# Batch 0's key-value products by head pairs, idle products in float32, and a second pair normalised on GpSimd

## The chip, the cores and the metric

The kernel runs on one core of one Trainium2 chip. The metric is the device time of one execution in microseconds (us); a lower one is better. A core has five engines that run their own instruction streams and wait for each other through semaphores: TensorE (PE in the profile, with its weight loads as PEld), VectorE (DVE), ScalarE (ACT), GpSimd (POOL) and SyncE (SP). Sixteen transfer engines (DMA) move data between memory and the core; transfers issued by SyncE are the queue "q1 hardware_dynamic" in the profile, those issued by GpSimd "q0 software_dynamic".

## The reference

Linear attention over 8 batches of 8 heads, 576 positions and 64 channels, followed by a two-layer network with a leaky ReLU, all in float32 at the interface:

```python
q_s = softmax of q over the channels
k_s = softmax of k over the positions
kv = np.einsum('bhsd,bhse->bhde', k_s, v)
x = np.einsum('bhsd,bhde->bhse', q_s, kv)        # (8, 8, 576, 64) -> tokens (4608, 512)
h = x @ w_in                                     # (512, 2048)
g = np.maximum(0.01 * h, h)
out = g @ w_out                                  # (2048, 512)
```

## The kernel before, in words

The 4608 tokens are worked off in nine tiles of 512. For each tile, 16 blocks of layer 1 (`layer1`, L521: four products over the channel blocks cb 0 to 3 of `w_in_sb`) are evicted through the leaky ReLU on ScalarE (L530), and then layer 2 (L542) multiplies them with `w_out_sb`. The attention of batch b+1 is prepared under the products of tile b, at places written out by hand with `at(tile, unit, ...)`. The order of instructions on every engine is the order of the program; nothing is rescheduled.

The change lies in the part before the first tile, L576 to L632, where batch 0's attention has nothing to hide under, and in `x1` at L771. A batch's eight heads lie in four pairs of partition halves: `hl` counts four heads per half, and a "pair" gg takes heads 2gg and 2gg+1 (called hp 0 and 1) in each of the two partition halves hh. One position row r of the nine holds 64 positions per half.

What is issued there, in order:

- SyncE loads q's first four rows (`RA`), k in two halves, v in two halves, and q's other rows (L93 to L96).
- `wake` and `wake_on` (L344, L350) run products on zeros or on a small tile, whose results nobody reads, into a PSUM tile of their own. `wake(14)` is first; others fill waits between the steps.
- GpSimd issues the first half of w_in (1024 of its 2048 columns, four pieces of 256 KB as stored, one for each cb) once k has landed: `load_w_in(0)`, L579. It casts v's first half (L593), normalises q's first rows of pair 0 (`q_first_norm`, L602), and then issues the second half of w_in, `load_w_in(1)`, L603.
- k's maximum over the positions goes through VectorE and TensorE (`k_tree`, `k_max_pe`, `k_all_dve`, `k_all_pe`), is subtracted (`k_sub_ps`, VectorE), and ScalarE takes the exponentials into `ke`.
- `kv_pair` (L389) multiplies `ke` with v, which carries a column of ones, for both heads and both halves: `kv_quads` issues, for each of nine rows, four products of 64 positions x 64 channels with 65 columns. The two results `pkv[hh]` lie in two PSUM banks, the two heads in the two halves of the partitions. The column of ones gives k's sum; `kd_rec` takes its reciprocal and `kd_one` writes the normalised result to `kd2` (VectorE).
- `q_turn_first` transposes q's first rows of a pair on TensorE, `q_keep_first` copies them to `qT`, `attend` (L444) multiplies with `kd2` and `x_keep` copies the result to `xT`, layer 1's input. Channel blocks 0 and 1 come from pair 0, blocks 2 and 3 from pair 1.
- For pair 0 VectorE keeps the transposes, for pair 1 ScalarE. Pair 1 is normalised on VectorE (L618).
- `q_max` and `q_sub` begin the softmax of rows 4 and 5 (`R1`) and 6 and 7 (`R2`), VectorE and GpSimd.

Then the first half (256 tokens) of tile 0 begins (L778 on): for the first eight blocks of layer 1 all products with cb 0, then `x1` (the attend of pair 1, its `x_keep`, and the exponentials of R1), then cb 1, 2 and 3. The other eight blocks need the second half of w_in; between their cb 0, 1 and 2 stand the transposes of R2's rows (`t2`), an attend of rows 4 to 7 (`x2`) and the first block of the second half of the tokens.

SyncE's next loads, batch 1's k and q, wait for the first piece of w_in's second half: `hold_sync(0, ...)` at L635 reads it first. GpSimd's later issues of w_out (`late_loads`, L640) wait for its third piece.

PSUM has eight banks: six rotate under one tag (`psB_pool`), two under another (`psO_pool`).

Of the kernel before, what the change touches and what calls it, by code (L numbers as in the profile page):

```python
# [8 lines left out]
FP32 = mybir.dt.float32  # L9
# [11 lines left out]
R = 9  # L21
# [4 lines left out]
def kernel(  # L26
# [68 lines left out]
    st[0]["v"] = load(v, 0, "v_raw", [(slice(0, 2), ALLR), (slice(2, 4), ALLR)])  # L95
    load(q, 0, "q_raw", [(ALLH, RB)], st[0]["q"])  # L96

    zero = const_pool.tile([P, TT], BF16)
    nc.gpsimd.memset(zero, 0.0)  # L99
    ident = const_pool.tile([P, P], BF16)  # L100
    make_identity(nc, ident)
# [9 lines left out]


    vb2 = [const_pool.tile([P, R, 2, 2, D + 2], BF16, name=f"vb{i}") for i in range(2)]
    kd2 = [const_pool.tile([P, 2, 2, D], BF16, name=f"kd{i}") for i in range(2)]
    for i in range(2):
        nc.gpsimd.memset(vb2[i][:, :, :, :, D : D + 1], 1.0)
# [1 line left out]

    w_in_r = moe_w_in.rearrange("(cb p) f -> p cb f", p=P)

    def load_w_in(fh):
        fs = slice(fh * (F // 2), (fh + 1) * (F // 2))
        for cb in range(NB):
            nc.gpsimd.dma_start(out=w_in_sb[:, cb, fs], in_=w_in_r[:, cb, fs])  # L124

    w_out_r = moe_w_out.rearrange("(fb f) o -> f fb o", f=P)
# [182 lines left out]
    def kv_quads(b, gg, outs, rs=ALLR):  # L309
        for r in range(R)[rs]:  # L310
            for hp in range(2):
                for hh in range(2):
                    rows = slice(hh * L, (hh + 1) * L)
                    nc.tensor.matmul(  # L314
                        outs[hh][hp * D : (hp + 1) * D, 0 : D + 1],
                        lhsT=st[b]["ke"][rows, r, 2 * gg + hp],
                        rhs=vb2[b % 2][rows, r, gg, hp, 0 : D + 1],
                        start=(r == 0),
                        stop=(r == R - 1),
                    )  # L320
# [20 lines left out]

    wake_ps = psO_pool.tile([P, TT], FP32, name="pout", tag="pout")

    def wake(n):  # L344
        for i in range(n):
            nc.tensor.matmul(  # L346
                wake_ps, lhsT=zero[:, 0:P], rhs=zero, start=(i == 0), stop=(i == n - 1)
            )

    def wake_on(a, n):  # L350
        for i in range(n):
            nc.tensor.matmul(
                wake_ps[0:RA.stop, 0:P], lhsT=a[:, HL - 1], rhs=identf, start=True, stop=True
            )

    def k_max_pe(b, i):
        ps = psB_pool.tile([P, 2, L], FP32, name="kT", tag=BANK_TAG)
# [28 lines left out]
        )  # L386

    def kv_pair(b, gg):
        pkv = [psB_pool.tile([P, D + 2], FP32, name="pkv1", tag=BANK_TAG) for _ in range(2)]  # L389
        kv_quads(b, gg, pkv)  # L390
        st[b]["pkv", gg] = pkv

    def kd_rec(b, gg, hh):
        st[b]["krec", gg, hh] = krec = small_pool.tile([P, 1], FP32, name="krec1")
        nc.vector.reciprocal(out=krec, in_=st[b]["pkv", gg][hh][:, D : D + 1])

    def kd_one(eng, b, gg, hh):
        pkv, krec = st[b]["pkv", gg][hh], st[b]["krec", gg, hh]
        eng.tensor_tensor(
            out=kd2[b % 2][:, gg, hh], in0=pkv[:, 0:D], in1=krec.to_broadcast([P, D]), op=ALU.mult  # L400
        )

    def q_transpose(b, r0, n, pool=psB_pool, tag=BANK_TAG):
# [22 lines left out]
    def cross(b, gg, outs, rows):  # L426
        for hp in range(2):
            for hh in range(2):
                half = slice(hp * D, (hp + 1) * D)
                if b == 1 and rows.start == RE.start:  # L430
                    rhs = st[b]["qE"].rearrange("c (r g) (h l) -> c g h r l", g=2, h=2)[:, gg, hh]
                elif "qX" in st[b]:
                    rhs = st[b]["qX"].rearrange("c (r g) (h l) -> c g h r l", g=2, h=2)[:, gg, hh, rows]
                else:
                    rhs = st[b]["qT"][:, 2 * hh + gg, rows]
                nc.tensor.matmul(  # L436
                    outs[hp][hh * D : (hh + 1) * D].rearrange("p (r l) -> p r l", l=L),
                    lhsT=kd2[b % 2][half, gg, hh],
                    rhs=rhs[half],
                    start=True,  # L440
                    stop=True,
                )
# [131 lines left out]


    HA, HB = slice(0, 1), slice(1, 2)  # L576
    wake(14)
    nc.gpsimd.tensor_copy(out=gate[:, 0:1], in_=st[0]["k"][:, HL - 1, R - 1, D - 1 : D])
    load_w_in(0)  # L579
    k_begin(0)  # L580
    q_begin(0)
    q_first(0, RA)
    wake_on(st[0]["nmax"], 4)
    k_tree(0, H0)
    k_max_pe(0, 0)
    wake(1)
    k_tree(0, H1, slice(0, 1))
    k_all_dve(0, 0)
    k_all_pe(0, 0)
    wake(2)  # L590
    k_tree(0, H1, slice(1, 4))
    nc.gpsimd.tensor_copy(out=gate[:, 0:1], in_=st[0]["kmax"][:, HL - 1, D - 1 : D])
    v_cast(nc.gpsimd, 0, 0)  # L593
    k_max_pe(0, 1)
    wake(1)
    k_sub_ps(0, 0, HA)
    k_exp(0, slice(0, 1))
    k_all_dve(0, 1)
    k_all_pe(0, 1)
    wake(3)  # L600
    q_first_rec(0, 0)
    q_first_norm(nc.gpsimd, 0, 0)  # L602
    load_w_in(1)  # L603
    k_sub_ps(0, 0, HB)
    k_exp(0, slice(1, 2))
    v_cast(nc.scalar, 0, 1)
    q_first_rec(0, 1)
    k_sub_ps(0, 1)
    k_exp(0, H1)
    kv_pair(0, 0)  # L610
    q_turn_first(0, 0)
    wake(3)
    kd_rec(0, 0, 0)
    kd_one(nc.vector, 0, 0, 0)
    q_keep_first(nc.vector, 0, 0)
    kd_rec(0, 0, 1)
    kd_one(nc.vector, 0, 0, 1)
    q_first_norm(nc.vector, 0, 1)  # L618
    attend(0, (0,), RA)
    for hp in range(2):  # L620
        x_keep(nc.scalar, 0, (0,), RA, hp)
    kv_pair(0, 1)
    q_turn_first(0, 1)
    q_keep_first(nc.scalar, 0, 1)
    q_max(0, R1)
    q_sub(nc.gpsimd, 0, R1)
    for hh in range(2):
        kd_rec(0, 1, hh)
        kd_one(nc.vector, 0, 1, hh)
    q_max(0, R2)  # L630
    q_sub(nc.gpsimd, 0, R2)
    load_w_out(slice(0, 2))  # L632


# [124 lines left out]
    def end_act(j, ph, half):  # L759
# [10 lines left out]
    )  # L770
    x1 = (  # L771
        lambda: attend(0, (1,), RA),
        lambda: x_keep(nc.vector, 0, (1,), RA, 0),
        lambda: q_exp(0, R1),
        lambda: x_keep(nc.scalar, 0, (1,), RA, 1),
    )

# [93 lines left out]
```

## The time and the profile before

| | us |
|---|---|
| median of 3 runs | 282.64 (282.36 to 283.31) |
| the profiled execution | 282.63 |
| its span, first to last instruction | 280.8 |

| engine | busy us | share of the span | instructions |
|---|---|---|---|
| TensorE, products | 273.7 | 97% | 2018 |
| TensorE, weight loads | 133.0 | 47% | 2018 |
| VectorE | 159.9 | 57% | 227 |
| ScalarE | 160.3 | 57% | 284 |
| GpSimd | 51.6 | 18% | 52 |

The granted clock of TensorE is 1.00 in every slice of the span. The transfer engines are busy 90% or more from about 7 us on in the first sixth of the span. Rows of the profile name an instruction by its line, engine and operation, the tile written and the tiles read, the sizes, how often it ran, and its mean time; the chain that ended last is followed back from the last instruction, at each step to what released it.

### The profile page before, as it was taken

The numbers are of one execution on the slowest core, as the hardware profiler recorded it, in microseconds if no ns is written. First come the engines' busy times: TensorE is split into PE (matmuls) and PEld (weight loads), VectorE is DVE, ScalarE is ACT, GpSimd is POOL, SyncE is SP. The second block draws the span as 40 slices with busy tenths as digits, with TensorE's granted clock in tenths as the row PEclk, the third lists the DMA queues.
The fourth block names the chain that finished last, engine by engine and source line by source line (L and its number), as shares of the span: only waits on it lengthen the run. The fifth ranks groups of instructions, "written<-read, shape, count | busy, mean of one in ns | idle before, by whom it ended". The sixth has DMA issues, their size and how long they took to land.

```text
span 280.8 us, 5005 instructions
## 1 busy us (share of the span) xinstructions
PE 273.7 (97%) x2018; PEld 133.0 (47%) x2018; DVE 159.9 (57%) x227; ACT 160.3 (57%) x284; POOL 51.6 (18%) x52
## 2 busy tenths in 40 slices
PE   8889999999999999999999999999999999999994
PEld 3378645444444544444444444444444444444443
DVE  3985897999999959956895598644600000000021
ACT  4975565784489177755586448644844364146400
POOL 2947280159005003000400070000000000000000
PEclk9999999999999999999999999999999999999999
DMA  7999999896692498099309930332033300330033
GB/s 246 332 209 319 247 261 398 265 377 198 194 396 94 90 362 292 1 255 394 92 2 255 400 84 0 84 77 58 20 84 75 71 6 0 75 77 0 0 75 77
DMA packets 37751, 45.94 MB, mean 164 GB/s; under 512 B 16608, under 2 KB 20960, under 8 KB 37728
## 3 DMA queue, kind: packets, MB, share of 16 engines
q1 hardware_dynamic: 34240, 41.30, 46.5%
q0 software_dynamic: 3328, 4.20, 8.5%
q8 instruction: 16, 0.26, 0.4%
q10 hardware_dynamic: 160, 0.13, 0.2%
q14 instruction: 7, 0.06, 0.1%
HBM read 36.70 MB, written 9.44 MB: 164 GB/s over the span
## 4 chain that ended last, share of the span: by engine, by line
PE 92%; DMA 5%; POOL 2%; SPq 0%; issue 0%; DVE 0%
PE pout L542 45%; PE ph L521 43%; DMA w_in_sb<-in_moe_w_in_dram 3%; DMA k_raw<-in_k_dram 2%; PE po L436 1%; PE pokv L314 1%; PE pkv L314 1%; POOL w_in_sb L124 1%; POOL vb L204 0%; SPq L81 0%; POOL qe L243 0%; PE psum_q L254 0%; PE pokv L436 0%; PE psum_qt L407 0%; DVE out_sb L536 0%
## 5 line engine op out<-in xcount | busy, mean ns | idle before, releaser
L542 PE MATMUL pout<-w_out_sb,gj 128*128 128x512 bf16 (+2 forms) x592 | 127.9, 374 | 0.0
L521 PE MATMUL ph<-xT,w_in_sb 128*128 128x512 bf16 (+1 forms) x640 | 126.6, 358 | 0.7 <-DMA w_in_sb<-in_moe_w_in_dram 0.7
L530 ACT ACTIVATE gj<-ph 128x512 bf16<-128x512 f32 x144 | 82.0, 602 | 26.9 <-PE ph L521 26.5
L521 PEld LDWEIGHTS <-w_in_sb 128*128 128x128 bf16 x640 | 62.3, 98 | 63.0 <-DMA w_in_sb<-in_moe_w_in_dram 0.9
L542 PEld LDWEIGHTS <-gj 128*128 128x128 bf16 x592 | 56.4, 98 | 64.9 <-issue 0.2
L536 ACT COPY out_sb<-pout 128x512 f32<-128x512 f32 (+1 forms) x29 | 16.8, 580 | 67.0 <-PE pout L542 46.2
L536 DVE COPY out_sb<-pout 128x512 f32<-128x512 f32 (+1 forms) x8 | 4.8, 638 | 70.8 <-PE pout L542 70.8
L204 POOL CAST vb<-v_raw 128x1152 bf16<-128x1152 f32 x13 | 22.8, 1781 | 81.3 <-DMA v_raw<-in_v_dram 67.0
L294 DVE TENSOR_REDUCE qsum<-qe 128x36 f32<-128x2304 bf16 (+5 forms) x13 | 20.0, 1541 | 9.8 <-ACT qe L285 9.6
L192 ACT ACTIVATE ke<-k_raw 128x2304 bf16<-128x2304 f32 (+2 forms) x11 | 17.6, 1598 | 10.8 <-DVE k_raw L184 10.7
L301 DVE TENSOR_TENSOR qe<-qe,qrec 128x2304 bf16<-128x2304 bf16 (+5 forms) x13 | 22.4, 1724 | 0.4
L215 DVE TENSOR_REDUCE qmax<-q_raw 128x36 f32<-128x2304 f32 (+5 forms) x13 | 20.0, 1537 | 0.7 <-DMA q_raw<-in_q_dram 0.7
L285 ACT ACTIVATE qe<-q_raw 128x2304 bf16<-128x2304 f32 (+5 forms) x13 | 17.2, 1320 | 3.0 <-POOL q_raw L277 3.0
L184 DVE TENSOR_TENSOR k_raw<-k_raw,kall 128x2304 f32<-128x2304 f32 (+1 forms) x8 | 17.2, 2164 | 0.3
L277 POOL TENSOR_TENSOR q_raw<-q_raw,qmax 128x512 f32<-128x512 f32 (+3 forms) x7 | 11.9, 1697 | 23.9 <-DVE qmax L215 19.1
L459 ACT CAST xT<-po 128x512 bf16<-128x512 f32 (+3 forms) x34 | 15.3, 540 | 1.5 <-PE po L436 1.5
L151 DVE TENSOR_TENSOR t<-t 128x256 f32<-128x256 f32 (+2 forms) x22 | 15.5, 706 | 0.7
L151 DVE TENSOR_TENSOR t<-k_raw 128x512 f32<-128x512 f32 (+1 forms) x11 | 12.1, 1102 | 2.2 <-DMA k_raw<-in_k_dram 1.9
L277 DVE TENSOR_TENSOR q_raw<-q_raw,qmax 128x2304 f32<-128x2304 f32 (+1 forms) x6 | 13.2, 2203 | 0.3
L334 DVE RECIPROCAL krec<-pokv 128x2 f32<-128x2 f32 x8 | 1.3, 165 | 20.8 <-PE pokv L436 20.8
L346 PE MATMUL pout<-zero 128*128 128x512 bf16 x24 | 8.4, 492 | 1.3 <-POOL zero L99 1.3
L314 PEld LDWEIGHTS <-ke 64*64 64x64 bf16 x576 | 6.7, 107 | 4.6 <-issue 2.5
(68 smaller groups left out, 106.4 us busy)
## 6 DMA issues: line engine op xcount, KB each, us to landing
out_dram<-out_sb SPq DMA_DIRECT2D x70, 128.0 KB, 2.9
q_raw<-in_q_dram SPq DMA_DIRECT2D x6, 1152.0 KB, 8.5
v_raw<-in_v_dram SPq DMA_DIRECT2D x6, 1152.0 KB, 11.0
k_raw<-in_k_dram SPq DMA_DIRECT2D x5, 1152.0 KB, 6.1
k_raw<-in_k_dram SPq DMA_DIRECT2D x6, 576.0 KB, 5.5
v_raw<-in_v_dram SPq DMA_DIRECT2D x4, 576.0 KB, 7.6
w_in_sb<-in_moe_w_in_dram POOLq DMA_DIRECT2D x8, 256.0 KB, 7.7
w_out_sb<-in_moe_w_out_dram POOLq DMA_DIRECT2D x8, 256.0 KB, 10.6
```

The lines of the kernel that those rows point to most:

```text
L151: nc.vector.tensor_tensor(out=o, in0=i0, in1=i1, op=ALU.max)
L184: eng.tensor_tensor(out=ks, in0=ks, in1=st[b]["kall"][:, hs].unsqueeze(2).to_broadcast([P, n, R, D]), op=ALU.subtract,)
L192: nc.scalar.activation(out=st[b]["ke"][:, :, hs].rearrange("p r h d -> p h r d"), in_=st[b]["k"][:, hs], func=AF.Exp,)
L204: eng.tensor_copy(out=o, in_=i)
L215: nc.vector.tensor_reduce(out=o, in_=st[b]["q"][:, hs, rs], axis=AX.X, op=ALU.max)
L277: eng.tensor_tensor(out=qs, in0=qs, in1=st[b]["qmax", rs.start, hs.start].unsqueeze(3).to_broadcast([P, m, n, D]), op=ALU.subtract,)
L294: nc.vector.reduce_sum(out=qsum, in_=st[b]["qe"][:, rs, hs], axis=AX.X)
L301: nc.vector.tensor_tensor(out=qes, in0=qes, in1=st[b]["qrec", rs.start, hs.start].unsqueeze(3).to_broadcast([P, n, m, D]), op=ALU.mult,)
L521: nc.tensor.matmul(ph, lhsT=w_in_sb[:, cb, j * P : (j + 1) * P], rhs=xT[:, cb, c0 : c0 + n], start=(cb == 0 and first), stop=(cb == NB - 1 ...
L530: nc.scalar.activation(out=o, in_=ph, func=AF.Prelu, alpha=LEAKY_SLOPE)
L536: copy(out=out_sb, in_=pout)
L542: nc.tensor.matmul(pout, lhsT=g_sb[j // 2][:, j % 2, tsub * P : (tsub + 1) * P], rhs=w_out_sb[:, j, os], start=(j == 0), stop=(j == NF - 1),)
```

## The change

- `zero` becomes a float32 tile of 128 columns. `wake` takes the numbers of columns of the float32 products that it runs, each reading one zero column again and again: 512, 512, 512 and 256 in place of 14 bf16 products of 512; 128, 256 and 384 in place of one, two and three. `wake_on` runs one float32 product of 512 columns in place of four of 128.
- `kv_pair` multiplies both heads of a pair at once: 64 positions x 128 channels with 130 columns, 18 products in place of 36 for each pair. Half of the result (one head's k with the other's v) is not used. `kd_one` normalises all of it into a tile of its own, `kd0`, and batch 0's attend reads the fitting quarter. Later batches go on with `kd2`.
- Pair 1 of q's first rows is normalised on GpSimd directly after pair 0, ahead of the issues of w_in's second half. These are split: pieces 0 and 1 there, piece 2 after `q_sub` of R1, piece 3 after `q_sub` of R2.
- R1's `q_max` and `q_sub`, pair 1's transposes and their copy (now VectorE) stand ahead of pair 0's `x_keep` and of `kv_pair(0, 1)`.
- In `x1` both `x_keep` are ScalarE's, and the exponentials of R1 stand ahead of them.

```diff
-    zero = const_pool.tile([P, TT], BF16)
+    zero = const_pool.tile([P, P], FP32)
...
+    kd0 = const_pool.tile([P, 2, 2, 2, D], BF16)
...
-    def load_w_in(fh):
+    def load_w_in(fh, cbs=slice(0, NB)):
         fs = slice(fh * (F // 2), (fh + 1) * (F // 2))
-        for cb in range(NB):
+        for cb in range(NB)[cbs]:
             nc.gpsimd.dma_start(out=w_in_sb[:, cb, fs], in_=w_in_r[:, cb, fs])
...
-    def wake(n):
-        for i in range(n):
+    def wake(*cols):
+        for n in cols:
             nc.tensor.matmul(
-                wake_ps, lhsT=zero[:, 0:P], rhs=zero, start=(i == 0), stop=(i == n - 1)
+                wake_ps[:, 0:n], lhsT=zero, rhs=zero[:, 0:1].to_broadcast([P, n]), start=True, stop=True
             )
 
-    def wake_on(a, n):
-        for i in range(n):
-            nc.tensor.matmul(
-                wake_ps[0:RA.stop, 0:P], lhsT=a[:, HL - 1], rhs=identf, start=True, stop=True
-            )
+    def wake_on(a):
+        nc.tensor.matmul(
+            wake_ps[0 : RA.stop], lhsT=a[:, HL - 1], rhs=zero[:, 0:1].to_broadcast([P, TT]), start=True, stop=True
+        )
...
     def kv_pair(b, gg):
-        pkv = [psB_pool.tile([P, D + 2], FP32, name="pkv1", tag=BANK_TAG) for _ in range(2)]
-        kv_quads(b, gg, pkv)
+        pkv = [psB_pool.tile([P, 2, D + 2], FP32, name="pkv1", tag=BANK_TAG) for _ in range(2)]
+        for r in range(R):
+            for hh in range(2):
+                rows = slice(hh * L, (hh + 1) * L)
+                nc.tensor.matmul(
+                    pkv[hh][:, :, 0 : D + 1],
+                    lhsT=st[b]["ke"][rows, r, 2 * gg : 2 * gg + 2].rearrange("p h d -> p (h d)"),
+                    rhs=vb2[b % 2][rows, r, gg, :, 0 : D + 1],
+                    start=(r == 0),
+                    stop=(r == R - 1),
+                )
...
-        nc.vector.reciprocal(out=krec, in_=st[b]["pkv", gg][hh][:, D : D + 1])
+        nc.vector.reciprocal(out=krec, in_=st[b]["pkv", gg][hh][:, 0, D : D + 1])
...
         eng.tensor_tensor(
-            out=kd2[b % 2][:, gg, hh], in0=pkv[:, 0:D], in1=krec.to_broadcast([P, D]), op=ALU.mult
+            out=kd0[:, gg, hh],
+            in0=pkv[:, :, 0:D],
+            in1=krec.unsqueeze(2).to_broadcast([P, 2, D]),
+            op=ALU.mult,
         )
...
-                    lhsT=kd2[b % 2][half, gg, hh],
+                    lhsT=kd0[half, gg, hh, hp] if b == 0 else kd2[b % 2][half, gg, hh],
...
-    wake(14)
+    wake(TT, TT, TT, 256)
...
-    wake_on(st[0]["nmax"], 4)
+    wake_on(st[0]["nmax"])
...
     q_first_norm(nc.gpsimd, 0, 0)
-    load_w_in(1)
     k_sub_ps(0, 0, HB)
     k_exp(0, slice(1, 2))
     v_cast(nc.scalar, 0, 1)
     q_first_rec(0, 1)
+    q_first_norm(nc.gpsimd, 0, 1)
+    load_w_in(1, slice(0, 2))
     k_sub_ps(0, 1)
     k_exp(0, H1)
     kv_pair(0, 0)
     q_turn_first(0, 0)
-    wake(3)
+    wake(384)
     kd_rec(0, 0, 0)
     kd_one(nc.vector, 0, 0, 0)
     q_keep_first(nc.vector, 0, 0)
     kd_rec(0, 0, 1)
     kd_one(nc.vector, 0, 0, 1)
-    q_first_norm(nc.vector, 0, 1)
     attend(0, (0,), RA)
+    q_max(0, R1)
+    q_sub(nc.gpsimd, 0, R1)
+    load_w_in(1, slice(2, 3))
+    q_turn_first(0, 1)
+    q_keep_first(nc.vector, 0, 1)
     for hp in range(2):
         x_keep(nc.scalar, 0, (0,), RA, hp)
     kv_pair(0, 1)
-    q_turn_first(0, 1)
-    q_keep_first(nc.scalar, 0, 1)
-    q_max(0, R1)
-    q_sub(nc.gpsimd, 0, R1)
     for hh in range(2):
         kd_rec(0, 1, hh)
         kd_one(nc.vector, 0, 1, hh)
     q_max(0, R2)
     q_sub(nc.gpsimd, 0, R2)
+    load_w_in(1, slice(3, 4))
     load_w_out(slice(0, 2))
...
         lambda: attend(0, (1,), RA),
-        lambda: x_keep(nc.vector, 0, (1,), RA, 0),
         lambda: q_exp(0, R1),
+        lambda: x_keep(nc.scalar, 0, (1,), RA, 0),
         lambda: x_keep(nc.scalar, 0, (1,), RA, 1),
```

More of the change, by code (lines that the diff above doesn't have):

```diff
@@ L582 @@
     q_first(0, RA)
-    wake_on(st[0]["nmax"], 4)
+    wake_on(st[0]["nmax"])
     k_tree(0, H0)
     k_max_pe(0, 0)
-    wake(1)
+    wake(P)
     k_tree(0, H1, slice(0, 1))
@@ L589 @@
     k_all_pe(0, 0)
-    wake(2)
+    wake(256)
     k_tree(0, H1, slice(1, 4))
@@ L594 @@
     k_max_pe(0, 1)
-    wake(1)
+    wake(P)
     k_sub_ps(0, 0, HA)
@@ L611 @@
     q_turn_first(0, 0)
-    wake(3)
+    wake(384)
     kd_rec(0, 0, 0)
```

## The prediction

> **What bounds the kernel now.** I read the page first: TensorE is busy 97% of the span at the full granted clock, so only the stretches where it waits can give anything. The chain that ended last, in order of time, then shows what ends those waits (columns: start, length, what):
>
> ```profile
> 1.79 5.77 DMA k_raw<-in_k_dram
> ...
> 10.26 1.08 POOL vb L204
> 11.34 0.81 POOL qe L243
> 12.15 0.11 issue
> 12.26 7.62 DMA w_in_sb<-in_moe_w_in_dram
> 19.88 0.05 issue
> 19.93 1.05 PE ph L521 x8
> ```
>
> From 19.93 us to the end the chain is TensorE alone (the page gives it 92% of the chain), and nothing of the change lies behind that point except what streams into it. So the question is one number: when can TensorE run the products of w_in's second half? There are four pieces of it, cb 0 to 3. They are needed at 19.93, 21.03, 22.34 and about 24.1 us (22.34 plus 16 products at the 0.109 us by which those starts are spaced), and landed at 19.88, 20.65, 21.88 and 23.12. TensorE had been ready for the first at about 19.05, four transposes after 18.82; the page gives its idle time there as 0.7 us.
>
> Next the transfers, in windows (columns: window, length, busy PE, PEld, DVE, ACT, POOL, then clock, DMA share, GB/s):
>
> ```profile
> 12.00:16.00 4.00, 3.75 (x99) 2.37 (x99) 3.86 (x13) 3.46 (x6) 3.32 (x6) 1.00 1.12 205
> 17.00:20.00 3.00, 2.28 (x24) 1.92 (x22) 2.86 (x6) 2.35 (x6) 1.11 (x2) 1.00 1.12 212
> 22.70:24.00 1.30, 1.30 (x15) 1.17 (x13) 1.23 (x3) 0.33 (x1) 1.30 (x3) 1.00 1.11 355
> ```
>
> The 16 transfer engines are full. The loads issued by SyncE fill them until 11.7 us, then w_in's eight 256 KB pieces follow in order at 205 GB/s, 1.28 us each, the second half from about 16.8. A piece issued at 12.26 therefore stood in line for some 4.5 us: the 7.62 us in the chain is queueing, not the price of an issue. The rise to 355 GB/s after 22.7 is batch 1's k, whose issue waits for cb 0.
>
> One more row, from the transfer queues between 17.5 and 19 us:
>
> ```profile
> q0 software_dynamic: 165, 0.30, 108.2%
> q8 instruction: 1, 0.02, 3.9%
> ```
>
> That instruction block of 16 KB started at 17.80 and took 0.94 us of one of the 16 engines. Fifteen of cb 0's 16 shares had landed by 18.76; the sixteenth came at 19.88. So the 0.7 us of idle TensorE is one instruction block in the way of one piece of weights.
>
> **The change, part by part.** The sum is made against the profiled run (282.63 us, span 280.8, the other 1.8 lying outside it); the median shown is 282.64, so a difference may be added to either.
>
> Idle products. The four float32 products of 128 columns (L352) leave eight records 0.11 us apart, 0.22 us a product; a bf16 product of 512 columns takes 0.21 (starts 5.94, 6.16, 6.37). So 14 x 512 bf16 columns equal (3 x 512 + 256) float32 columns, and wake(1), (2), (3) equal 128, 256, 384; wake_on stays at 0.87. Cost 0. The memset of zero falls from 0.52 to 0.20 (row of identf's memset), so the products start 0.3 us sooner, in front of a wait for nmax that ends after 6 us anyway: 0. What does change is the count. With two records per float32 product, TensorE's loads and products up to the first attend fall from 164 to 104, and kv_pair(0,1) has 36 in place of 72.
>
> Head pairs. No 64x128 product is in the trace. In L314's burst four 64x64 products start every 31 ns, so all four quarters work at once. With 130 columns and the two row halves still side by side, nine steps of about 57 ns (a transpose of 128 columns, L254, is spaced 55) make 0.51 us in place of 0.28: +0.23 a pair. If the halves take turns it is 1.03, +0.75. I take +0.23, since row halves side by side are what L314 shows, and keep +0.75 for the range. Each kd then writes 128 columns: 0.29 (row of L335) for 0.22 (L399), +0.07 four times.
>
> VectorE up to the first attend. It was busy with the k subtraction until 12.79, so krec moves only from 12.75 to 12.97; with the kd of each half the second one ends at 14.20 instead of 13.84, and attend follows 0.36 later. The normalisation that leaves (0.68, L243 DVE) gives this back to what follows: q_max of R1 ends at 14.8 instead of 15.04. On GpSimd the same work costs 1.07 (L243 POOL), at 12.34 to 13.4, and its result is first wanted at 14.4: hidden, with 1 us to spare. Queued behind it on GpSimd are the w_in issues.
>
> Second pair. Its four transposes (0.22) move ahead of kv_pair(0,1), which runs 14.65 to 15.33 for 14.34 to 14.82. Its kd's end at 16.26 for 15.70, the second attend is 0.56 late (16.51 for 15.95), and the 24 products that close the first half end 0.56 late. x_keep on ScalarE in place of VectorE (0.35 for 0.42) ends near 17.2, wanted at 17.6: hidden. TensorE is ready for cb 0 at 19.6 instead of 19.05, still ahead of the old 19.93. So 0.56 of the idle 0.7 is spent, and that costs nothing as long as the transfers stay the bound.
>
> The issues. Pieces 0 and 1 leave GpSimd at 13.33 and 13.9 instead of 12.26 and 12.85. Piece 2 waits behind q_sub(R1): 14.9 + 1.04 = 15.9. Piece 3 waits behind q_sub(R2), whose q_max ends at 16.85: 16.93 + 1.04 = 17.9 instead of 13.88, and w_out's first issue follows it. The trace shows GpSimd's queue twice being restarted: from 7.74 (issue) to 11.29 (first data) and from 22.45 to 26.48, so 3.55 and 4.03 us, both beside full traffic. By 3.55 piece 0's data starts at 16.9 (queue free about 16.7), piece 2's at 19.45 (about on time), piece 3's at 21.45 instead of 20.65. Piece 3 then lands 0.8 late at 23.9, which is still before the 24.1 at which it was used. By 4.03 its data starts at 21.9, the last third runs beside batch 1's k at half rate (from 26.6 to 30 us the two queues took 59% and 54% of the engines), and it lands at 24.9: +0.8. At the other end, if a running queue answers at once, nothing is late. I take 3.55, the row of the same pieces.
>
> The Trainium skill, page "DMA: Bandwidth & Descriptors", section on latency and other measured facts, puts the first byte of such a transfer at about 1 us after issue. By that piece 3 would be in line in time and the sum would be the gain alone, near 282.3; the two rows above are three to four times longer, though under full load, and the sum goes by the rows.
>
> The instruction block. If its request follows the count of TensorE's instructions, the point passed at about 12.5 us before (record 141, in the first kv burst) comes at about 14.9, inside the second kv burst, and the block runs at some 20 us instead of 17.8. It then hits piece 2 and not piece 0: cb 0 lands near 18.9, cb 1 near 20.2, cb 2 near 22.4 (21.27 plus the same 1.1). TensorE starts cb 0 at 19.6 (0.33 gained), cb 1 at 20.7, and waits again for cb 2 until 22.4, where it was before (22.34). The stall moves from one piece to another and the end hardly moves.
>
> Sum: between -0.3 (the gain kept) and +0.8 (piece 3 late). Likeliest 0 to 0.1: **282.7 us**, its own range 282.2 to 283.4.
>
> **The rivals.**
> (1) Slower, the late pieces decide. From the point where piece 3's data starts after 21.6 us, landing replaces need: 4.03 us and half rate give 24.9 against 24.1, 283.4; half a microsecond later on GpSimd (a q_max that waits for its kd's) doubles in the shared stretch and gives 284.0. Taking the chain at its word, 7.62 us after an issue moved by 1.07, also gives 283.7. For it: both restart rows. Against it: the line in front of the pieces.
> (2) Slower, the row halves take turns: +0.52 more on each kv pair, TensorE ready at 20.6, piece 3 issued near 18.9. Both together 283.5 to 284.2. Against it: L314's four at once.
> (3) Slower, the idle products don't hold the clock, so the first half's 32 products run at the 0.43 us per 512 columns seen before 5.5 us: 0.104 us more for each of 256 columns, 3.3 in all, less the 0.33 of slack: 285.6. Against it: L352's float32 products ran at full rate.
> (4) Faster: the block falls behind all four pieces, GpSimd's queue answers in under 3 us, and the head pairs cost no more than the 0.28 they replace. TensorE is then ready at 19.0, cb 0 is there at 18.8, and 0.9 to 1.1 is gained: 281.6. For it: the instruction count does fall by a third. Against it: it needs all three.
>
> **How the numbers follow.** Forecast 0.45; (1) 0.22, (2) 0.10, (3) 0.03, (4) 0.20. The range 281.6 to 284.0 reaches to (4) and through (1) and most of (2). Faster or slower by over 0.3% (0.85 us, about what a measurement of this kernel can tell from no change) takes (4) on one side and (1) to (3) on the other: 0.20, 0.45, 0.35.
>
> **What would show it.** Right: kv bursts of about 0.7 us, kd rows of 0.29, the first w_in issue of the second half at 13.3 and the fourth near 17.9, the 16 KB block at 19.5 to 20.5, and TensorE's wait at cb 2 or cb 3 instead of cb 0, about as long as before. Wrong: a gap in GpSimd's queue of over 0.5 us with TensorE waiting at cb 3 (rival 1), bursts over 1 us (2), products at 0.21 us per 256 columns after 8 us (3), or no wait at all after 19 us (4).

## The result and the profile after

The changed kernel takes 283.41 us (median of 11 runs, 282.45 to 284.75) where the kernel before takes 282.64 (11 runs, 282.23 to 283.31): a ratio of 1.0034, 95% interval 1.0023 to 1.0045 (the medians themselves differ by 0.77 us, 0.27%). It is slower by about 0.3%. The profiled execution took 283.15 us with a span of 281.4, against 282.63 and 280.8, so 0.6 us of the loss can be looked for in the two traces.

The chain of waits of the changed kernel, in order of time (start, length, what):

```profile
15.72 6.91 DMA w_in_sb<-in_moe_w_in_dram
22.62 0.03 issue
...
22.75 0.18 POOL gate L655
22.93 0.28 issue
23.21 2.80 POOL w_out_sb L130 x4
26.01 14.68 DMA w_out_sb<-in_moe_w_out_dram
40.69 0.04 issue
40.73 2.75 PE pout L554 x12
```

Before, the chain was TensorE alone from 19.93 us. Now it stays with the transfers until 40.69: through piece cb 2 of w_in's second half, through the gate by which GpSimd holds back w_out until cb 2 has landed, and through the fifth of the w_out issues behind that gate (rows 10 and 11). TensorE's own list says how long it waited for the first of the two (timeline: start, length, engine, line, operation, tiles; in brackets the idle time before and what ended it):

```profile
12.10 0.70 PE L393 MATMUL pkv<-vb,ke 64*128 64x130 bf16 x18 [0.16 <-ACT ke L193]
...
14.67 0.70 PE L393 MATMUL pkv<-vb,ke 64*128 64x130 bf16 x18
...
19.43 1.04 PE L533 MATMUL ph<-xT,w_in_sb 128*128 128x256 bf16 x8
...
20.65 1.04 PE L533 MATMUL ph<-xT,w_in_sb 128*128 128x256 bf16 x8
21.61 0.41 PE L448 MATMUL po<-qT,kd 64*64 64x256 bf16 x8
22.67 1.59 PE L533 MATMUL ph<-xT,w_in_sb 128*128 128x256 bf16 x13 [0.64 <-DMA w_in_sb<-in_moe_w_in_dram]
```

The first piece is used at 19.43 instead of 19.93, half a microsecond sooner. The third is used at 22.67 instead of 22.34: all of the gain and 0.33 us more are gone. From cb 2's first product to the w_out product of rows 10 and 11 TensorE needs 17.77 us where nothing stops it (22.88 to 40.65 and 22.43 to 40.20 in two kernels further down), so it could have run that one at 40.44; it ran at 40.73, when the rows had landed (40.68). 0.33 + 0.29 = 0.62 us, which is the difference of the spans.

The transfers between 19 and 23 us (window: length, busy PE, PEld, DVE, ACT, POOL, then clock, DMA share, GB/s), first of the kernel before:

```profile
19.00:23.00 4.00, 3.28 (x38) 2.48 (x36) 1.93 (x5) 2.47 (x5) 0.72 (x2) 1.00 1.14 210
```

and of the changed kernel:

```profile
19.00:23.00 4.00, 3.36 (x39) 2.48 (x37) 2.60 (x6) 2.90 (x6) 0.43 (x2) 1.00 1.01 167
```

The engines look nearly as busy (1.01 for 1.14), but they moved a fifth less: 43 GB/s for 4 us, 0.17 MB, which at 210 GB/s is 0.8 us of transfer time. Inside the window, in slices of 0.15 us, the rate falls from some 205 GB/s to 123 to 157 at 20.35 us and is back near 200 at 23.5:

```profile
GB/s 191 246 205 191 218 205 205 191 246 123 137 123 123 150 150 137 143 157 150 123 137 137 150 150 150 184 164 154 152 190 200 246 283 243 314 360 323 372 403 382
```

(19 to 25 us). The kernel before in the same slices:

```profile
GB/s 205 191 259 205 218 205 205 191 205 219 219 191 218 205 218 205 178 178 198 212 212 218 205 198 222 212 344 355 357 420 382 398 398 422 369 430 369 369 399 399
```

The loss does not end at 23 us. Two shorter windows, first of the kernel before:

```profile
20.50:22.50 2.00, 2.00 (x27) 1.47 (x25) 0.44 (x2) 0.47 (x2) 0.22 (x2) 1.00 1.15 204
22.50:24.50 2.00, 2.00 (x20) 1.80 (x19) 1.43 (x3) 0.53 (x1) 2.00 (x3) 1.00 1.13 351
```

and of the changed kernel:

```profile
20.50:22.50 2.00, 1.53 (x20) 0.98 (x20) 0.82 (x2) 1.25 (x3) 0.00 (x0) 1.00 0.93 139
22.50:24.50 2.00, 1.83 (x17) 1.59 (x18) 1.05 (x3) 0.15 (x1) 1.47 (x3) 1.00 1.12 223
```

In the second window batch 1's k was already running before the change, while cb 3 and w_out's first piece still moved after it. From 19 to 25 us together 203 GB/s stand against 270, 0.40 MB, so the 0.8 us is only the part up to 23 us. The first half of batch 1's k landed 1.2 us late (27.04 for 25.85), although SyncE issued it 0.9 us sooner (19.68 for 20.57).

When each piece had landed, from the records of the transfers (15th of the 16 shares, then the last):

| piece | before | changed |
|---|---|---|
| w_in second half, cb 0 | 18.76, 19.88 | 18.98, 19.00 |
| cb 1 | 20.03, 20.65 | 20.30, 20.32 |
| cb 2 | 21.27, 21.88 | 21.54, 22.62 |
| cb 3 | 22.52, 23.12 | 24.18, 24.35 |
| w_out rows 6 and 7 | 33.71, 33.78 | 34.66, 35.09 |
| w_out rows 10 and 11 | 38.76, 38.84 | 40.44, 40.68 |

Two things are in this table. First, the sixteenth share that is 1.1 us late has moved from cb 0 to cb 2: the instruction block of 16 KB now runs from 20.28 for 0.98 us. It stands in the transfer queues between 20 and 21.5 us (queue, packets, MB, share of 16 engines):

```profile
q0 software_dynamic: 122, 0.22, 89.8%
q8 instruction: 1, 0.02, 4.1%
```

In the same lines before, around the block, the software queue had 108.2%; here it has 89.8%. Second, from cb 2 on everything is late, cb 3 by 1.2 us and w_out by up to 2.1 (rows 8 and 9: 38.01 for 35.93). The next instruction block has a part in the last figure, since it came at 27.17 before and at 32.02 here; against the kernel with one issue further down, whose blocks lie nearly as here (20.30 and 31.76), it is 1.8 (38.01 for 36.22).

What exactly slowed the queue is not shown. That it was short of work is a reading; when the rate fell at 20.35, cb 3 (17.97) and w_out's first piece (18.53) had been issued. cb 3's first share was also in time: it had landed at 21.83, against 21.77 before. Only then did the shares spread, the first fifteen over 2.35 us (21.83 to 24.18) instead of 0.75 (21.77 to 22.52). The records of single packets say the same: between 20.5 and 22.5 us fewer were started (162 of 1 KB and more, for 277), most still took no longer than before, and eight took 0.3 to 1.2 us, where before none was over 0.2.

### The profile page after: what moved, and what is told of

It is laid out like the page before. It is cut to its first block, busy times and chain, and to the rows that moved or that the text cites. A ratio compares the mean times of both kernels' runs of the same rounds, so it can differ in the third digit from the quotient of the medians.

```text
span 281.4 us, 4909 instructions
## 1 busy us (share of the span) xinstructions
PE 275.0 (98%) x1970; PEld 134.1 (48%) x1970; DVE 159.9 (57%) x226; ACT 160.1 (57%) x284; POOL 49.6 (18%) x53
## 4 chain that ended last, share of the span: by engine, by line
PE 84%; DMA 9%; DVE 3%; POOL 1%; issue 0%; ACT 0%; SPq 0%; POOLq 0%
PE pout L554 42%; PE ph L533 39%; DMA w_out_sb<-in_moe_w_out_dram 5%; DMA w_in_sb<-in_moe_w_in_dram 2%; DMA k_raw<-in_k_dram 2%; PE po L448 1%; POOL w_out_sb L130 1%; DVE t L152 1%; PE pokv L315 1%; PE pkv L315 1%; DVE k_raw L384 0%; POOL q_raw L278 0%; PE pkv L393 0%; ACT ke L193 0%; DVE kmax L152 0%
## 5 line engine op out<-in xcount | busy, mean ns | idle before, releaser
L205 POOL CAST vb<-v_raw 128x1152 bf16<-128x1152 f32 x13 | 20.2, 1582 | 83.9 <-DMA v_raw<-in_v_dram 83.9
L278 POOL TENSOR_TENSOR q_raw<-q_raw,qmax 128x512 f32<-128x512 f32 (+3 forms) x7 | 11.9, 1696 | 24.1 <-DVE qmax L216 24.1
L152 DVE TENSOR_TENSOR t<-k_raw 128x512 f32<-128x512 f32 (+1 forms) x11 | 11.2, 1015 | 3.7 <-DMA k_raw<-in_k_dram 3.5
L335 DVE RECIPROCAL krec<-pokv 128x2 f32<-128x2 f32 x8 | 1.3, 164 | 20.6 <-PE pokv L448 20.6
L347 PE MATMUL pout<-zero 128*128 128x512 f32 (+3 forms) x18 | 9.2, 637 | 1.0 <-POOL zero L99 1.0
L315 PEld LDWEIGHTS <-ke 64*64 64x64 bf16 x504 | 5.9, 107 | 3.6 <-issue 2.1
```

The lines of the kernel that those rows point to most:

```text
L152: nc.vector.tensor_tensor(out=o, in0=i0, in1=i1, op=ALU.max)
L205: eng.tensor_copy(out=o, in_=i)
L278: eng.tensor_tensor(out=qs, in0=qs, in1=st[b]["qmax", rs.start, hs.start].unsqueeze(3).to_broadcast([P, m, n, D]), op=ALU.subtract,)
```

## The experiments

Two theories stood against each other. **The split**: pieces cb 2 and cb 3, issued behind q_sub on GpSimd, reach the queue too close to their turn, the queue runs at two thirds of its rate meanwhile, and w_out and batch 1's loads pay. **The block**: what counts is which piece the instruction block falls on, and the split is hidden. The other parts (idle products, head pairs, GpSimd's normalisation) could each be rivals too. Ratios are to the kernel before, on the same chip, with their 95% intervals.

### The block alone, moved to an earlier place (kernel before)

```
-    wake(14)
+    for _ in range(56):
+        nc.tensor.matmul(wake_ps[:, 0:P], lhsT=zero[:, 0:P], rhs=zero[:, 0:P], start=True, stop=True)
```

> The kernel before, with the first 14 idle bf16 products of 512 columns cut into 56 of 128: the same columns, 84 more instruction records of TensorE ahead of everything else. Theory (an instruction block in the way of a weight piece sets the wait): the block is requested by count, so it runs at about 14 to 15 us instead of 17.8, through the first half of w_in; cb 0 lands at 18.8 to 19.4 instead of 19.88, TensorE starts it 0.4 to 0.8 earlier, 281.8 to 282.3. Rival (the block has no part in it, the transfers are just that slow): cb 0 at 19.9, 282.6.

282.36 us, ratio 0.9995 (0.9985 to 1.0004). The block moved to 16.36 us (14 to 15 expected), onto cb 3 of the first half, for which TensorE then waited 0.26 us (to 18.45). It started cb 0 of the second half at 19.56 instead of 19.93 and cb 2 at 21.97 instead of 22.34, as the theory has it, and the 0.37 us were lost again 20 us later. The timeline of this kernel:

```profile
40.92 1.15 ACT L202 CAST vb<-v_raw 128x1152 bf16<-128x1152 f32 x1 [1.48 <-DMA v_raw<-in_v_dram]
41.98 1.16 ACT L192 ACTIVATE ke<-k_raw 128x1152 bf16<-128x1152 f32 x1
42.62 1.05 PE L314 MATMUL pkv<-vb,ke 64*64 64x65 bf16 x72
```

Batch 1's 72 key-value products, 0.78 us before, now stretch over 1.05: the second half waits for ScalarE's exponentials, which wait for batch 1's v from memory. In the kernel before the same activation ended at 42.86 and the products began at 42.80, so there was no slack behind the front at all. What is gained at the front is worth nothing without an earlier batch 1.

### The idle products alone in float32 (kernel before)

```
-    zero = const_pool.tile([P, TT], BF16)
+    zero = const_pool.tile([P, P], FP32)
...
-    wake(14)
+    wake(TT, TT, TT, 256)
```

with the other wake calls as in the change.

> The kernel before with one part of the change alone: the idle products in float32 (wake and wake_on, the tile zero). Theory of the block: TensorE counts some 30 records fewer, the block moves from 17.8 to 19 to 20 us and hits cb 1 or cb 2 in place of cb 0; TensorE starts cb 0 at 19.1 and waits at cb 1 or cb 2; 282.4 to 282.8, the same within 0.2. Rival (float32 idle products cost time by themselves, by clock or by length): the first half's products start later or run slower, over 283.

282.44 us, 0.9998 (0.9989 to 1.0006). The block moved to 18.34 (19 to 20 expected) and fell on cb 1 (20.94); TensorE started cb 0 at 19.45 and cb 2 at 22.31, where it was. The clock stayed at 1.00. The idle products cost nothing, as predicted.

### The changed kernel with the four pieces in one issue

```
-    load_w_in(1, slice(0, 2))
+    load_w_in(1)
...
-    load_w_in(1, slice(2, 3))
...
-    load_w_in(1, slice(3, 4))
```

> The changed kernel with the four pieces of w_in's second half issued together, at 13.1 to 15.3 us, ahead of q_sub of R1. Theory of the block: cb 2 still lands near 22.6 because the block at about 20.3 is still there, so TensorE's wait at cb 2 stays (0.3 against the kernel before); cb 3 and w_out come earlier, so the second wait near 40.7 goes: 282.9 to 283.1. Rival (the split, late issues make cb 2 and cb 3 late): both waits go, 282.3 to 282.5. A third outcome, q_sub of R1 a microsecond later holding up the exponentials of R1: 283.4 or more.

282.81 us, 1.0017 (0.9999 to 1.0035). The window of 19 to 23 us:

```profile
19.00:23.00 4.00, 3.85 (x44) 2.90 (x43) 2.61 (x6) 3.14 (x6) 0.21 (x2) 1.00 1.15 209
```

209 GB/s, as before the change. The block still fell on cb 2 (20.30; landed 22.39, used at 22.43, 0.09 us later than before), and w_out's rows 10 and 11 landed at 39.06 and were no longer waited for (40.20). So in the profiled executions the second of the two losses, and most of the first, go with the split. The times alone do not decide it: the interval holds both no change and most of the change's loss, and the 12 runs reach from 282.50 to 285.41.

### The split alone, in the kernel before

```
-    load_w_in(1)
+    load_w_in(1, slice(0, 2))
...
     q_sub(nc.gpsimd, 0, R1)
+    load_w_in(1, slice(2, 3))
...
     q_sub(nc.gpsimd, 0, R2)
+    load_w_in(1, slice(3, 4))
```

> The kernel before with one part of the change alone: w_in's pieces 2 and 3 of the second half issued after q_sub of R1 and after q_sub of R2. Theory (the late issues leave the software queue short of work from 20 to 23 us, everything behind it, w_out above all, lands later): its bytes by 23 us fall from 2.34 to about 2.2 MB, w_out's piece 5 lands after 40 us in place of 38.84; the time 282.8 to 283.3. Rival (only the instruction block and the longer chain of the head pairs count): 282.5 to 282.7.

283.34 us, 1.0031 (1.0018 to 1.0045), 282.62 to 284.98 in 11 runs: as much as the whole change loses, with as wide a scatter, from this part alone. The profiled execution was the quickest of them (282.62), and shows the mark but little of its price:

```profile
19.00:23.00 4.00, 3.85 (x43) 2.75 (x41) 2.36 (x6) 2.54 (x5) 0.76 (x3) 1.00 1.06 183
```

Rows 10 and 11 landed at 40.14 and were used at 40.18. That is 0.43 us later than cb 2's first product (21.98) plus 17.77 us, and it used up the 0.36 us by which cb 2 had been used sooner than in the kernel before. That the other executions lost more at this point is likely and was not profiled.

### The block moved to an earlier place in the changed kernel

```
+    zb = const_pool.tile([P, P], BF16)
+    nc.gpsimd.memset(zb, 0.0)
     zero = const_pool.tile([P, P], FP32)
...
-    wake(TT, TT, TT, 256)
+    for _ in range(56):
+        nc.tensor.matmul(wake_ps[:, 0:P], lhsT=zb, rhs=zb, start=True, stop=True)
```

> The changed kernel with its first idle products as 56 bf16 products of 128 columns: the same columns, some 100 more records early. Theory of the block: it runs at about 15 us, cb 2 lands at 21.5 to 22.1 instead of 22.6, TensorE's wait at cb 2 goes or shrinks to 0.2, cb 3 lands near 24 and may bind instead by some tenths: 282.5 to 283.0. Rival (split issues): the wait at cb 2 stays, 283.4.

284.39 us, 1.0071 (1.0055 to 1.0086), far from both expectations. The block moved to 16.55, cb 2 was used at 22.32 without a wait, and the kernel got slower. TensorE now waits twice for transfers, first 0.44 us for cb 3, as the expectation had allowed (landed at 24.63, used at 24.68), then for w_out (its waits in total, times and longest; then the timeline):

```profile
PE pout L556 <- DMA w_out_sb<-in_moe_w_out_dram: 0.9, 1, 0.9
PE ph L535 <- DMA w_in_sb<-in_moe_w_in_dram: 0.4, 1, 0.4
...
39.83 1.89 PE L556 MATMUL pout<-w_out_sb,gj 128*128 128x512 bf16 x8 [0.93 <-DMA w_out_sb<-in_moe_w_out_dram]
```

The next block of 16 KB ran at 28.74 among the w_out pieces; from there on the sixteenth share of each came 1.5 to 1.7 us behind the fifteenth (30.11 and 31.62, 38.08 and 39.79). The front's queue had run at 160 GB/s between 19 and 23 us, so w_out had no reserve. The block on cb 2 is therefore not the main cause: with it gone, TensorE no longer waits there, and the kernel is slower. How the 0.93 us divide between the late queue and the second block, this run does not say; the next one differs from it in the split alone.

### Both together: one issue and the block earlier

The edits of the kernel with one issue and of the kernel just above, together.

> The changed kernel with the four pieces issued together and the first idle products as 56 bf16 products of 128 columns, some 100 records more. Theory of the block: it runs near 16.5 us, cb 2 lands by 21.9 and TensorE doesn't wait there; what is gained at the front (0.2) is eaten at batch 1's key-value products, which wait for ke until about 42.9: 282.4 to 282.8. If the second block falls among w_out's pieces (28 to 29 us) and these have no slack: 283 or more, with the wait near 40 us.

282.52 us, 0.9998 (0.9989 to 1.0007). 209 GB/s between 19 and 23 us, cb 2 used at 22.26 without a wait, w_out used at 40.02. Batch 1's key-value products came at 42.71, against 42.80 before, behind the exponentials that ran from 41.78. The second block ran at 26.71, among the w_out pieces again, and cost nothing. The change without its split and without the block on cb 2 equals the kernel before, and the split put back into this kernel costs 1.9 us (284.39).

### One issue, and the old products of 64 by 64

The kernel with one issue of four pieces, with kv_pair, kd_rec and kd_one as before the change.

> The changed kernel with the four pieces issued together, and with the old products of single heads, kd_one and kd2 as well. If the head pairs cost 0.2 to 0.4 on the chain but lie under the transfers: TensorE ready for cb 0 some 0.3 to 0.4 earlier (19.3), then a wait for cb 0, 1 or 2 by where the instruction block falls, the same time as with head pairs within 0.3: 282.5 to 283.0. If the head pairs are on the path: 0.4 faster or more, 282.3 or less.

282.66 us, 1.0000 (0.9990 to 1.0010). With the head pairs it was 1.0017 (0.9999 to 1.0035); the two intervals overlap. The instruction count changed with them, so the block went back to 18.09 and onto cb 0 (20.10); TensorE waited there (0.34) instead of at cb 2 (0.15). The head pairs' longer bursts (0.70 for 0.48 us) leave no cost that can be told from this.

### An attempt to beat both

```
-    wake(14)
+    for _ in range(70):
+        nc.tensor.matmul(wake_ps[:, 0:102], lhsT=zero[:, 0:P], rhs=zero[:, 0:102], start=True, stop=True)
...
-    lambda: v_cast(nc.scalar, 1, 1),
+    lambda: v_cast(nc.gpsimd, 1, 1),
```

> The kernel before with 70 idle products of 102 columns in place of 14 of 512 (112 more records, the same columns) and batch 1's second cast of v on GpSimd instead of ScalarE. Theory: the first block runs near 14.5 us, cb 0 lands near 19.2 and TensorE starts it 0.6 to 0.7 earlier; batch 1's key-value products, which held e1 to the old time, find ke some 0.7 earlier and keep it: 281.9 to 282.3. Rival (the end is set elsewhere): 282.5.

282.91 us, 1.0012 (1.0000 to 1.0024): it is not faster than either. The block moved to 14.23, cb 0 was used at 19.64, and ke was ready sooner (its last activation ran from 41.10), but the key-value products then waited for another copy on ScalarE (0.36 us, qT) and came at 43.08.

### How late is too late

Three kernels vary the split. First, the changed kernel with only cb 3 late:

```
-    load_w_in(1, slice(0, 2))
+    load_w_in(1, slice(0, 3))
...
-    load_w_in(1, slice(2, 3))
```

> The changed kernel with pieces cb 0 to 2 of w_in's second half issued together and only cb 3 left behind q_sub(R2). Theory (the queue runs short because cb 3's issue, near 18, comes too close to the moment its turn comes): the stretch at 120 to 150 GB/s between 20 and 23 us stays, w_out's rows 10 and 11 land at 40.5 or later, 283.2 to 283.5. Rival (the loss grows with the number of late pieces, or is due to cb 2's issue at 15.7): half of it or none, 282.7 to 283.0.

283.97 us, 1.0058 (1.0039 to 1.0077), 282.94 to 285.62 in 8 runs. The window:

```profile
19.00:23.00 4.00, 3.77 (x43) 2.84 (x42) 2.61 (x6) 3.14 (x6) 0.70 (x2) 1.00 0.99 163
```

So the loss does not grow with the number of late pieces: one late piece is enough, and it is not less than with two. cb 3 was issued at 18.23 and its first share had landed at 22.20. The rate was 103 to 159 GB/s from 20.5 to 23 us, so that cb 2, issued long before, was slow as well: the queue slows down while the piece ahead of the late one moves, although the late one had been issued 2 us earlier. The time came out above what was expected.

Second, the changed kernel with cb 2 and cb 3 issued together behind q_sub(R1):

```
-    load_w_in(1, slice(2, 3))
+    load_w_in(1, slice(2, 4))
...
-    load_w_in(1, slice(3, 4))
```

> The changed kernel with cb 2 and cb 3 issued together behind q_sub(R1), near 15.7 and 16.3, ahead of q_sub(R2). Theory (an issue some 5 us ahead of its turn is soon enough): over 200 GB/s all the way from 19 to 23 us, cb 3's 15 shares by 23.4, w_out's rows 10 and 11 by 39.5, and the time of the kernel with one issue of four pieces, 282.6 to 282.9. Rival (any split of the issue costs, through GpSimd's order): 283.1 to 283.5.

282.99 us, 1.0013 (0.9997 to 1.0029), 282.54 to 283.55 in 8 runs.

```profile
19.00:23.00 4.00, 3.58 (x41) 2.68 (x39) 2.46 (x6) 3.17 (x7) 0.19 (x2) 1.00 1.12 192
```

The two issues began at 16.16 us, and most of the rate and of the time is back. The expectation was a little too good: 192 GB/s and not over 200 throughout, cb 3's 15 shares by 23.63, rows 10 and 11 at 39.66, where they were not waited for. The profiled execution (283.12) lost 0.54 us at cb 2 (used at 22.88). Both causes are in this: cb 2's fifteenth share came at 22.42, 1.15 us later than before the change, and its sixteenth, behind the block at 20.80, at 22.84; TensorE waited 0.42 us, the time between the two. w_out's loss is absent.

Third, the kernel before with cb 2 and cb 3 both behind q_sub(R2):

```
-    load_w_in(1)
+    load_w_in(1, slice(0, 2))
...
     q_sub(nc.gpsimd, 0, R2)
+    load_w_in(1, slice(2, 4))
```

> The kernel before with cb 2 and cb 3 both issued behind q_sub(R2), near 17.7 and 18.3: a larger dose of the late issue alone. Theory: data of cb 2 starts near 21.3 where the queue is empty from about 20; cb 2 lands after 22.6 and TensorE waits for it 0.5 to 1 us, cb 3 lands near 24.5, w_out follows 1 us late: 283.6 to 284.2. Rival (what counts is only where the instruction block falls): as with cb 3 alone late, 283.0 to 283.4.

283.94 us, 1.0055 (1.0038 to 1.0073). The window, and two lines of TensorE's timeline:

```profile
19.00:23.00 4.00, 3.58 (x40) 2.52 (x38) 2.06 (x5) 2.60 (x6) 0.71 (x3) 1.00 1.04 160
```

```profile
21.12 1.05 PE L521 MATMUL ph<-xT,w_in_sb 128*128 128x256 bf16 x8 [0.37 <-DMA w_in_sb<-in_moe_w_in_dram]
...
38.77 1.89 PE L542 MATMUL pout<-w_out_sb,gj 128*128 128x512 bf16 x8 [0.51 <-DMA w_out_sb<-in_moe_w_out_dram]
```

The time is as the split theory had it; the places differ. cb 2's data came early enough (22.29, used at 22.44), since the slow stretch had come one piece sooner: it was cb 1, the piece ahead of the late ones, that ran at 82 to 177 GB/s between 19.15 and 20.65 us; its last share came at 21.07, the block (18.66) having fallen on it as well. The main price was paid at w_out again, here two rows sooner.

### w_out issued sooner

The changed kernel, with the gate in front of w_out's seven later issues on cb 1 instead of cb 2:

```
-        nc.gpsimd.tensor_copy(out=gate[:, 0:1], in_=w_in_sb[:, 2, F - 1 : F])
+        nc.gpsimd.tensor_copy(out=gate[:, 0:1], in_=w_in_sb[:, 1, F - 1 : F])
```

> The changed kernel with the seven later issues of w_out held until cb 1 instead of cb 2 has landed, some 2 us sooner. Theory (the second part of the loss is paid at w_out's rows 10 and 11): they land by 40.2 or sooner, TensorE doesn't wait for them, the wait at cb 2 stays; 282.8 to 283.2, and less scatter from run to run. Rival (what w_out gains batch 1's k, q and v lose at the shared engines, so TensorE waits at batch 1's products instead): 283.3 or more.

284.83 us, 1.0110 (1.0075 to 1.0145): the rival, and more of it. The seven issues began at 21.47 instead of 23.21. The chain of this kernel:

```profile
22.20 11.02 DMA q_raw<-in_q_dram
...
37.62 2.73 POOL q_raw L278
40.35 3.45 POOL k_raw L185
43.80 0.02 issue
43.83 1.17 ACT ke L193
45.00 0.04 issue
45.05 0.48 PE pkv L315 x36
```

The first half of batch 1's q landed at 33.22 instead of 31.27, everything that GpSimd and ScalarE do for batch 1 followed, and its key-value products ended 1.3 us later than in the changed kernel. Rows 10 and 11 themselves landed at 41.02, no sooner. From 23 to 43 us w_out and batch 1's loads share the engines and neither has slack: in this kernel the transfers that the split loses were shifted from the one to the other, not won back. The kernels with one issue avoid the loss where it arises, in the queue before 23 us.

### All of them side by side

| kernel | GB/s, 19 to 23 us | time, ratio |
|---|---|---|
| before | 210 | 1 |
| before, block earlier | 217 | 0.9995 |
| before, float32 idle products | 208 | 0.9998 |
| changed, one issue, block earlier | 209 | 0.9998 |
| changed, one issue, 64 by 64 | 207 | 1.0000 |
| before, block earlier, a cast moved | 210 | 1.0012 |
| changed, one issue | 209 | 1.0017 |
| changed, cb 2 and 3 behind R1 | 192 | 1.0013 |
| before, split alone | 183 | 1.0031 |
| changed | 167 | 1.0034 |
| changed, cb 3 alone late | 163 | 1.0058 |
| before, cb 2 and 3 behind R2 | 160 | 1.0055 |
| changed, block earlier | 160 | 1.0071 |
| changed, w_out sooner | 173 | 1.0110 |

The rate is that of one profiled execution each, the ratio that of 5 to 12 runs. Every kernel that keeps over 205 GB/s is within 0.2% of the kernel before, every one under 185 is 0.3% slower or more.

## Why the prediction was right, and where it was not

The time, 283.41, lies in the range and in the likeliest case's own range (282.2 to 283.4) but for 0.01; it is at the prediction's bound of 0.3% (the ratio, 1.0034, just beyond it, the difference of the medians, 0.77 us, just below its 0.85). That the kernel is slower at all was not the forecast, whose likeliest case was 0 to 0.1 us; the time is inside the range because the range had room for rivals. Step by step:

- **Idle products, cost 0.** Right: 0.9998 alone, clock 1.00. Rival (3) falls with it.
- **Head pairs, 0.51 for 0.28.** Right in mechanism and size: 18 products with their pipeline take 0.70 us where 0.71 follows from the forecast (0.48 for the old burst, plus the 0.23), so the row halves work side by side, and rival (2) falls. kd took 0.29 us as forecast.
- **VectorE and the second pair.** Right: the second attend's products start at 16.28 (16.51 forecast), TensorE came to cb 0 at 19.43 (19.6).
- **The issues.** The times were right (13.13, 13.7, 15.72 and 17.97, for 13.33, 13.9, 15.9 and 17.9). cb 3's shares came between the two cases worked out, 24.35 for 23.9 and 24.9. The need for it had moved to 24.41 (22.67 plus 16 products), so it was late by 1.2 us and yet not waited for, by 0.06 us. The working behind it did not hold. It took the 3.55 us of a restart as the delay of each piece and had cb 3's data start at 21.45. But cb 3's first share had landed at 21.83, and at this rate a share takes about 1.2 us (cb 1's first landed at 19.25, cb 2's at 20.49), so its data started near 20.6, in line. Late were the other shares. In the kernel with cb 2 and 3 behind R2 the same reading failed: cb 2's data was expected near 21.3, and its first share had landed at 20.92.
- **The block.** Right: 20.28 for "some 20", onto cb 2, used at 22.67. The step gave 22.4 for its landing because it took the full rate; the fifteenth share was at 21.54 instead of 21.27, the block's 1.08 came on top, and 22.62 is the sum.
- **The step that failed** is "Piece 3 then lands 0.8 late at 23.9, which is still before the 24.1 at which it was used." The sentence closes the account too soon. It asks when the late piece itself is wanted, not what stands beside and behind it. The queue ran at two thirds of its rate for 2 to 3 us (139 GB/s for 204), and cb 2 in front of the late piece was slow as well: its fifteenth share came 0.27 us late, and with the block behind it TensorE was 0.33 us behind the kernel before. cb 3, batch 1's k and q and most of w_out landed 0.9 to 2.1 us late, and at w_out's rows, which had no slack left, another 0.29 us was paid in the profiled execution and more in others (w_out in the kernel with the block earlier: 0.93). The sum had put both at nothing. The prediction had even read the proof of the shared stretch, the two queues at 59% and 54%, and used it for cb 3 alone. "Nothing of the change lies behind that point except what streams into it" was the place to go on.
- **Rival (1)** said that the late pieces decide, and gave 283.4. They do, but in the changed kernel not through TensorE waiting for cb 3, which was its point of decision; that wait came only in the kernel with the block earlier (0.44 us), where cb 2 no longer hid it. That 283.4 is also the measured time is luck: the price was worked out from a wait that did not occur. Its second figure does not add up by its own words, since half a microsecond doubled is 1.0 and gives 284.4, not 284.0. The split alone gives 283.34, the change without it 282.81 or, with the block out of the way as well, 282.52.
- **Rival (4)** wanted the block behind all four pieces. Where the front did get quicker (0.37 us in the kernel before with the block earlier), the gain vanished at batch 1's key-value products; the 281.6 was out of reach for a reason that the prediction did not have.

The prediction cited the Trainium skill, page "DMA: Bandwidth & Descriptors", section "Latency and other measured facts": a first byte about 1 us after issue. By that rule the split would have been free, and it was not (283.34 for the split alone). The figure itself is not settled by cb 3: from its issue to its first landed share 3.9 us passed (17.97 to 21.83), and 4.0 in the kernel with cb 3 alone late (18.23 to 22.20), but in this time the piece also stood behind cb 2 and moved itself. Where GpSimd's queue ran dry (at 25.91 in the changed kernel, beside batch 1's loads), its next data came 4.0 us after the issue (23.21 to 27.19), as in the prediction's rows; there the trace does not agree with the page.

What stays open: first, by what mechanism a late issue slows the pieces ahead of it, as said above. Second, why single executions of the split kernels take over 2 us more than their quickest; one of the kernel with one issue did so too (285.41 for 282.50). No such execution was profiled; that w_out is then later still is likely from the above and not shown.

## What to carry to other kernels

A late transfer is not judged by when its own data is wanted: follow the queue to everything behind it, up to the first point with slack. Pieces that still stand in front are no proof that an issue is early enough. Here cb 3, issued 3.3 us before cb 2 would have been through (17.97 against 21.27), had cb 1 and cb 2 in front of it and cost a fifth of the rate between 19 and 23 us (167 GB/s for 210). Issues 3.9 us or more ahead (cb 2 at 16.16 against cb 1's 20.03, cb 3 at 16.73) cost a tenth (192), and all four together nothing (209). So in a kernel like this, weights should be issued before work on the same engine and not between it. And before tuning a wait at the front, look for the next meeting point (here batch 1's key-value products at 42.8 us): without slack there, a gain in front is lost again.

## What the runs showed of the hardware

- **A late issue cost rate before its own turn came, and the engines did not look idle.** In the changed kernel the engines' busy share from 20.5 to 22.5 us was 0.93 at 139 GB/s, against 1.15 at 204 before: each busy microsecond moved a sixth less. The rate fell while the piece ahead of the late one was moving, one piece before the gap that one would look for.
- **Where an instruction block falls moved with the number of instructions that TensorE had run:** 14.23 us with 70 short idle products, 16.4 to 16.6 with 56, 17.8 to 18.7 where the 64 by 64 products stand beside either form of the idle products of the two kernels, and 20.3 to 20.8 with the change's head pairs and float32 products. In all fourteen kernels TensorE had started 128 to 163 loads and products 5.3 us before the block began. That the count is the cause fits this; it is not all of it, since the same products gave 17.80, 18.01 and 18.66 in three kernels. The block takes one of 16 engines for 0.93 to 1.1 us and delays the sixteenth share of the piece in hand by about as much. The Trainium skill, page "Runtime: NRT & Kernel Launch", section "Instruction fetch mechanics", says that instructions are fetched in blocks of 16 KiB over a DMA queue, at a cost that is mostly hidden. The size agrees; hidden it was in most places, and not where the piece in hand was awaited (0.64 us of TensorE at cb 2) or where the queue had no reserve (1.5 to 1.7 us a piece among w_out's).
- **Products of 64 rows by 128 columns of weights** run two at a time on TensorE's row halves: 18 of them with 130 columns each in 0.70 us, twice in the changed kernel, started in pairs (nine pairs from 14.67 to 15.15 us).
